# RWKV attention followed by a normalized two-layer MLP on one core: r of the first twelve tiles loaded in long runs and turned by small selection products, rstd on ScalarE, and a new order of the work

## The chip, the cores and the metric

One core of one Trainium2 chip runs the whole program. The metric is device microseconds from start to end of one launch. Five engines work side by side, each with a queue of its own: TensorE (PE, with its weight loads shown apart as PEld), VectorE (DVE), ScalarE (ACT), GpSimd (POOL) and SyncE (SP, which here only issues DMAs). Transfers run on 16 DMA engines.

## The reference

There are 4 batches, 8 heads, 768 steps and a head dimension of 48. Each head carries a 48 x 48 state that decays by w per step; the result, put into rows of 384, goes through a layer normalization with a gain and a two-layer MLP with a residual.

```python
def _attn_ref(r, k, v, w, u):
    for t in range(S):
        cur = np.einsum('bhd,bhe->bhde', u[None] * kt, vt)
        y[:, :, t] = np.einsum('bhd,bhde->bhe', rt, state + cur)
        state = w[None, :, :, None] * state + np.einsum('bhd,bhe->bhde', kt, vt)
...
def _moe_ref(x, g_ln, w_ch1, w_ch2):
    mu = np.mean(x, axis=-1, keepdims=True)
    var = np.mean((x - mu) ** 2, axis=-1, keepdims=True)
    xn = (x - mu) / np.sqrt(var + 1e-06) * g_ln
    ch = np.maximum(xn @ w_ch1, 0.0) @ w_ch2
    return (x + ch).astype(np.float32)
```

w_ch1 is 384 x 1536 and w_ch2 is 1536 x 384. All inputs and the output are float32; the kernel multiplies in bfloat16.

## The kernel before, in words

The sequence is cut into 6 chunks of 128 steps. With 4 batches this makes 24 tiles; tile i is chunk i // 4 of batch i % 4. Tiles 0 to 3 need no state, and tile i reads the state that tile i - 4 left.

**The attention part of a tile.** LR, LK and LV (L328, L325, L331) load r, k and v of the tile with the time step on the partition, all 8 heads side by side: 128 x 8 pieces of 48 float32 numbers, 192 bytes each. SR and SK multiply r by w to the power t (Fr) and k by w to the power -(t+1) (Fk) and write bfloat16, each head padded to 64 (tile sc; L194). TR turns the scaled r and k, four 128 x 128 transposes each, on TensorE (L348), and TC, TCr and TCk copy them from PSUM into trs. From tile 12 on TKR does this turning by a DMA transpose instead (K_BY_DMA, L497). AT multiplies turned k with turned r per head (L371, 48 rows of the array, the two heads of a pair on its two halves), AM masks the result (L381), Q multiplies r by k elementwise, and S forms the u term (L402) and the new state's sum of k times v (L415). CC, ZU and ZD take these out of PSUM, VB multiplies v by the u term per head (L434), Y adds state times r (L444) and A times v (L452), and X adds Vb and gives the sum of each row (L459).

**The MLP part.** SQ gives the squared deviation of a row (L466), XN the centred row in bfloat16, LT or LT2 turns it (TensorE or DMA), UP is the first layer (L527), RL its relu out of PSUM (L543, L545), DN the second layer (L557), OT scales by the row's rstd and adds x (L615), and STO stores. RS makes rstd on GpSimd with a multiply-add (L480) and a power of -0.5 (L483). GROUPS says which tiles go through the first layer together: single tiles for 0 to 5 and 20 to 23, pairs between. The first layer's weights are loaded in thirds (LW1, L301) and scaled by -g to bfloat16 (SW, L308 and L312); the second layer's come into the same three buffers later (LW2, CW).

**The order.** PLAN is a list of steps "name, tile, engine or place". It is issued in this order by hand, so each engine's queue holds its own steps of the list in the order of the list; v, s and g mean VectorE, ScalarE and GpSimd, and h, p, o and a are PSUM pools. SLOTS gives the number of buffers of each ring. All loads and most stores are issued by SyncE, one after the other. DU steps are products of zeros that only keep TensorE busy.

Of the kernel before, what the change touches and what calls it, by code (L numbers as in the profile page):

```python
# [17 lines left out]
PLAN = """
LR,1,- LK,0,- MI,0,g MW,0,v WF,0,s WB,0,- LC,0,s LC,1,s MM,0,g MP,0,v TL,0,s LC,2,s DU,21,h LN,0,s FK,0,s FR,0,s SK,0,v LK,1,- LR,0,- SK,1,v CT,0,o
DU,7,h SR,0,v TR,0,h TCk,0,s SR,1,v TR,1,h TCk,1,v TCr,0,s Q,0,v AT,0,- CP,0,s WL,0,s LR,2,- SR,2,g TCr,1,v LK,2,- SK,2,g TR,2,h AMb,0,v AMa,0,v  # L20
AT,1,- LV,1,- LK,3,- AMb,1,v AMa,1,v UW,0,g TCk,2,s TCr,2,s AT,2,- AMb,2,v UGC,0,s LV,0,- CV,0,s S,0,h CC,0,v VB,0,v ZU,0,v Y,0,h X,0,v XN,0,v LR,3,-
CV,1,s Q,1,g SK,3,g SR,3,g TR,3,- Q,2,g S,1,o CC,1,v VB,1,g ZU,1,v AMa,2,v Y,1,- X,1,v LK,5,- LR,4,- SR,4,g TCr,3,s TCk,3,s AT,3,- Q,3,v AM,3,v LV,2,-
CV,2,s S,2,h CC,2,s ZU,2,v LT,0,o XN,1,s XT,0,s LK,4,- LR,5,- SR,5,v VB,2,v SK,4,g DU,3,p TR,4,- TC,4,v Q,4,v LV,3,- CV,3,s S,3,o CC,3,s SQ,1,s ZU,3,v
LV,4,- SK,5,g TR,5,- TC,5,s VB,3,g Y,2,- X,2,v LT,1,- XT,1,s XN,2,s CV,4,g S,4,h ZU,4,v CC,4,s LV,5,- CV,5,g ATP,4,- AM,4,v LW1,0,- SW,1,s Y,3,h
SQ,0,s X,3,v XN,3,s SQ,2,s LT,2,h XT,2,v Q,5,g S,5,- AM,5,v ZU,5,v Y,4,o SW,2,g SW,0,g UP,16,- RL,16,s LW1,2,- SW,6,s CC,5,s LT,3,- XT,3,s UP,32,-
RL,32,s UP,0,- RL,0,s LW1,1,- SW,5,s VB,4,g X,4,v XN,4,v SW,7,g SW,8,g UP,2,o RL,2,v VB,5,g UP,48,p RL,48,v Y,5,h SW,3,g LK,6,- SK,6,v X,5,v UP,18,-
RL,18,s XN,5,s SW,4,g UP,49,p RL,49,s UP,33,o LR,7,- SR,7,v UP,34,- RL,34,s LK,7,- SK,7,g RS,2,g RL,33,v UP,17,- RL,17,s TR,7,p TC,7,s RS,0,g LT,5,h
XT,5,v LT,4,- UP,1,o LR,6,- Q,7,v LW2,2,- UP,82,- SR,6,g TR,6,- UP,81,- XT,4,s RL,1,v LV,7,- CV,7,v CW,5,v S,7,- CC,7,v ZU,7,v CW,4,g DN,6,- RL,82,v
TC,6,s Q,6,g ATP,6,- AM,7,v AM,6,v LW2,1,- CW,2,s SQ,4,s DN,2,p UP,50,- RL,50,s CW,3,g DN,5,- VB,7,g DN,1,- RL,81,v Y,7,h LW2,0,- CW,1,s CW,0,g DN,4,-
DN,0,- SQ,5,s RS,1,g OT,1,v LV,6,- CV,6,s S,6,h CC,6,s LK,9,- SK,9,g UP,66,o SQ,3,s X,7,v XN,7,g SQ,7,s VB,6,g ZU,6,v RL,66,v UP,64,- RL,64,s Y,6,h  # L30
LR,9,- SR,9,v LR,8,- SR,8,g DN,10,- RS,5,g TR,9,- X,6,v XN,6,s LK,8,- SK,8,v DN,8,- OT,0,v TR,8,- TC,8,v Q,8,v TC,9,s Q,9,v RS,3,g RS,4,g DN,9,-
OT,2,v UP,65,- RL,65,s ATP,8,- UP,80,p AM,9,v LV,9,- CV,9,g LR,10,- SR,10,g DN,18,- S,9,h ZU,9,v DN,17,- CC,9,v LK,10,- SK,10,g LV,8,- CV,8,s S,8,h
LR,11,- SR,11,v CC,8,v RL,80,s ZU,8,v VB,9,g TR,10,- AM,8,v TC,10,v VB,8,g LT2,6,- UP,96,- RL,96,s Q,10,v UP,98,p RL,98,s UP,97,- RL,97,s Y,9,h X,9,v
# [629 lines left out]
```

## Time and profile before

| what | us |
|---|---|
| three runs, median | 148.81 (148.49 to 149.31) |
| profiled execution | 148.24 |
| its span | 146.5 |
| TensorE busy in the span | 135.8 |
| VectorE busy | 110.5 |
| GpSimd busy | 94.0 |
| ScalarE busy | 80.1 |
| DMA queue of SyncE, share of 16 engines | 86.3% |

The span runs from the first to the last instruction of the core. Instructions of DMA issue, branches and semaphores are not counted as busy. In a row of a timeline the first number is the start and the second the duration; xN says how many instructions are merged in it. In a row of the chain of waits the second number is the piece of the chain. In a row of the groups, "busy, mean ns" stands behind the count, then the idle time ahead of the group and what ended it. In a row of a stretch stand the length, then busy time and number of instructions of TensorE, its weight loads, VectorE, ScalarE and GpSimd, then the granted clock of TensorE, the DMA share and GB/s.

### The profile page before, as it was taken

To read this page: it belongs to the slowest core of one execution; us is meant where nothing else is said; L and a number is where in the kernel's file an instruction comes from. 1 tells how busy PE (TensorE), PEld (TensorE's weight loads), DVE (VectorE), ACT (ScalarE), POOL (GpSimd) and SP (SyncE) were. 2 spreads that over 40 slices of the span, in tenths; PEclk is the share of its full clock that TensorE was granted. 3 is DMA by queue.
4 is the path that set the end of the run, shared out by engine and by line. 5 is a ranking of instruction groups with operands and counts; after the bars stand their busy time and mean duration, and the time that the engine had idled before them with its cause. 6 is when DMAs were issued, how large, how long until landed. Compare 5 with 4: busy or idle time off the path is not lost.

```text
span 146.5 us, 4250 instructions
## 1 busy us (share of the span) xinstructions
PE 135.8 (93%) x1693; PEld 108.2 (74%) x1693; DVE 110.5 (75%) x220; ACT 80.1 (55%) x175; POOL 94.0 (64%) x132
## 2 busy tenths in 40 slices
PE   3966699999999999999999999999999999999991
PEld 1455477998687897787688887966877777888871
DVE  4569999767969899985959948897946796875232
ACT  2575577977676467466386560663654752244600
POOL 4089878967888999989957493428553076644030
PEclk9999556999999999999999999999999999999999
DMA  5999899999889999899999999988999997830114
GB/s 97 209 211 221 175 277 401 194 258 380 231 170 188 206 197 232 156 215 242 96 229 206 260 233 186 217 166 185 245 157 199 229 184 156 206 123 0 54 37 182
DMA packets 99267, 28.59 MB, mean 195 GB/s; under 512 B 94508, under 2 KB 97712, under 8 KB 99248
## 3 DMA queue, kind: packets, MB, share of 16 engines
q1 hardware_dynamic: 98352, 27.24, 86.3%
q10 hardware_dynamic: 896, 1.09, 2.0%
q8 instruction: 13, 0.21, 0.6%
q14 instruction: 6, 0.05, 0.1%
HBM read 18.88 MB, written 4.72 MB: 161 GB/s over the span
## 4 chain that ended last, share of the span: by engine, by line
PE 60%; SPq 11%; DMA 11%; DVE 7%; POOL 6%; issue 4%; DVEq 0%; POOLq 0%
PE hp L527 17%; PE o L557 16%; PE s L557 7%; PE s L527 5%; SPq L332 4%; DMA w_f<-in_moe_w_ch_dram 4%; SPq L329 4%; SPq L326 3%; DMA trs<-sc 3%; DMA rf<-in_r_dram 3%; PE o L527 3%; PE at L371 2%; PE hp L452 2%; POOL sc L194 2%; PE at L348 2%
## 5 line engine op out<-in xcount | busy, mean ns | idle before, releaser
L527 PEld LDWEIGHTS <-w_sb 128*128 128x128 bf16 x612 | 47.9, 114 | 2.4 <-POOL w_sb L312 0.4
L527 PE MATMUL hp<-xT,w_sb 128*128 128x128 bf16 (+1 forms) x408 | 39.9, 244 | 0.3 <-POOL w_sb L312 0.3
L557 PEld LDWEIGHTS <-hT 128*128 128x128 bf16 x276 | 25.2, 97 | 13.7 <-issue 0.4
L557 PE MATMUL o<-w_sb,hT 128*128 128x384 bf16 x180 | 34.5, 326 | 0.0
L543 ACT ACTIVATE hT<-hp 128x512 bf16<-128x512 f32 x41 | 24.3, 597 | 18.2 <-PE hp L527 17.7
L381 DVE TENSOR_TENSOR A<-at,mask 128x1024 bf16<-128x1024 f32 (+1 forms) x27 | 28.9, 1096 | 1.2 <-PE at L371 1.2
L194 POOL TENSOR_TENSOR sc<-kf,Fk 128x384 bf16<-128x384 f32 x14 | 14.5, 1044 | 10.5 <-DMA kf<-in_k_dram 10.4
L434 POOL TENSOR_TENSOR Vb<-vf,cc 128x384 f32<-128x384 f32 x17 | 14.7, 868 | 8.7 <-ACT cc L189 3.6
L557 PE MATMUL s<-w_sb,hT 128*128 128x384 bf16 x96 | 18.9, 326 | 0.2 <-DVE x L459 0.2
L194 POOL TENSOR_TENSOR q<-trs 128x512 bf16<-128x512 bf16 x11 | 13.4, 1220 | 5.5 <-PE hp L527 2.6
L194 POOL TENSOR_TENSOR sc<-rf,Fr 128x384 bf16<-128x384 f32 x12 | 13.0, 1082 | 5.3 <-DMA rf<-in_r_dram 5.3
L466 ACT ACTIVATE sqj<-x,sm 128x384 bf16<-128x384 f32 x24 | 14.7, 611 | 1.4 <-DVE x L459 1.3
L615 DVE SCALAR_TENSOR_TENSOR ot<-o,rs,x 128x384 f32<-128x384 f32 x15 | 9.2, 613 | 4.5 <-POOL rs L483 2.8
L459 DVE SCALAR_TENSOR_TENSOR x<-hp,Vb 128x384 f32<-128x384 f32 x19 | 10.5, 554 | 2.3 <-PE hp L452 1.6
L483 POOL TENSOR_TENSOR rs<-rs,expo 128x1 f32<-128x1 f32 (+1 forms) x17 | 10.6, 625 | 1.4
L472 ACT ACTIVATE xn<-x,sm 128x384 bf16<-128x384 f32 x13 | 8.0, 613 | 5.7 <-DVE x L459 5.6
L371 PE MATMUL at<-trs 48*128 48x128 bf16 x192 | 8.6, 229 | 2.4 <-ACT trs L189 1.2
L527 PE MATMUL s<-xT,w_sb 128*128 128x128 bf16 (+1 forms) x120 | 10.8, 235 | 0.0
L194 POOL TENSOR_TENSOR Z<-ZS,WLZ 128x384 bf16<-128x384 f32 x10 | 10.3, 1030 | 0.6 <-DVE ZS L428 0.6
L545 DVE TENSOR_SCALAR hT<-hp 128x512 bf16<-128x512 f32 x9 | 6.2, 689 | 4.6 <-PE hp L527 4.6
L371 PEld LDWEIGHTS <-trs 48*128 48x128 bf16 x192 | 6.0, 99 | 4.9 <-ACT trs L189 2.1
L194 DVE TENSOR_TENSOR sc<-rf,Fr 128x384 bf16<-128x384 f32 x12 | 7.5, 633 | 2.3 <-DMA rf<-in_r_dram 2.2
(116 smaller groups left out, 214.3 us busy)
## 6 DMA issues: line engine op xcount, KB each, us to landing
rf<-in_r_dram SPq DMA_DIRECT2D x24, 192.0 KB, 3.8
kf<-in_k_dram SPq DMA_DIRECT2D x24, 192.0 KB, 3.9
vf<-in_v_dram SPq DMA_DIRECT2D x24, 192.0 KB, 3.9
w_f<-in_moe_w_ch_dram SPq DMA_DIRECT2D x6, 768.0 KB, 7.2
out_dram<-ot SPq DMA_DIRECT2D x18, 192.0 KB, 3.4
out_dram<-ot ACTq DMA_DIRECT2D x5, 192.0 KB, 2.0
trs<-sc SPq DMA_TRANSPOSE x12, 3.9
xT<-xn SPq DMA_TRANSPOSE x9, 2.8
```

The costliest lines, as they stand in the source:

```text
L194: engines[e].tensor_tensor(out=out, in0=in0, in1=in1, op=ALU.mult)
L371: nc.tensor.matmul(out=t[:, par, q, :], lhsT=trs(i)[p0 : p0 + D, 1, q, :], rhs=trs(i)[p0 : p0 + D, 0, q, :], start=True, stop=True,)
L381: nc.vector.tensor_tensor(out=AA(i)[:, a:b].rearrange("p e q t -> p (e q) t"), in0=psum["at", i][:, a:b].rearrange("p e q t -> p (e q) t") ...
L434: engines[e].tensor_tensor(out=Vb(i)[:].rearrange("p (h d) -> p h d", h=H), in0=vf(i)[:], in1=cc(i)[:].unsqueeze(2).to_broadcast([P, H, D] ...
L459: nc.vector.scalar_tensor_tensor(out=xx(i)[:], in0=psum["y", i][:, :C], scalar=1.0, in1=Vb(i)[:], op0=ALU.mult, op1=ALU.add, accum_out=sm[ ...
L466: nc.scalar.activation(out=sqj[:], in_=xx(i)[:], func=ACT.Square, bias=sm[i][:], scale=-float(C), accum_out=sq[g][:, j : j + 1])
L472: nc.scalar.activation(out=xn(i), in_=xx(i)[:], func=ACT.Identity, bias=sm[i][:], scale=-float(C))
L483: nc.gpsimd.tensor_tensor(out=rs[g][:], in0=rs[g][:], in1=expo[:, :n], op=ALU.pow)
L527: nc.tensor.matmul(out=t[:, a * gw : (a + 1) * gw].rearrange("p (j t) -> p j t", j=size), lhsT=w1_sb[n][kc][:, fb::FB], rhs=xT(g)[:, :size ...
L543: nc.scalar.activation(out=o, in_=s, func=ACT.Relu)
L557: nc.tensor.matmul(out=psum["o", i][:, :C], lhsT=hT(g)[:, fk, j * P : (j + 1) * P], rhs=w2_sb[d][:, a, :], start=(seen == 0 and a == 0), s ...
L615: nc.vector.scalar_tensor_tensor(out=ot(i), in0=psum["o", i][:, :C], scalar=rs[g][:, j : j + 1], in1=xx(i)[:], op0=ALU.mult, op1=ALU.add,)
```

## The change

**r of tiles 0 to 11.** LP loads r of two batches of one chunk at once. The partition now holds batch, head and one of 8 blocks of 16 steps, so each of 128 pieces is 16 steps x 48 = 768 numbers, 3072 bytes, contiguous. SP scales it by Fq, w to the power t laid out that way, which WS, LNQ, FA and FQ make at the start (w spread over partitions by a product with a selection matrix, its logarithm, times t, exp). TP turns it: for each of the 16 steps in a block, four products with 64 rows and 64 columns of the array pick the heads of one batch and parity out of the identity (32 moving columns each), 64 products per pair of tiles, into float32 PSUM. TCr copies the result of a tile into trs in the order of time. k of these tiles is turned alone (TK, KC). Heads are paired as h and h + 4 instead of 2q and 2q + 1, which changes the access patterns of SK, SR, CV, CC and Y, not their counts.

**rstd and Vb.** RS becomes two activations on ScalarE, Ln and Exp. VB may run on ScalarE as eight activations, one per head; seven tiles do so.

**The order.** PLAN is written anew; DU is 24 and 8 instead of 21, 7 and 3.

```diff
+PACK = 16
+R_PACKED = 12
-SLOTS = {'kf': 11, 'rf': 11, 'vf': 11, ...}
+SLOTS = {'kf': 10, 'sp': 2, 'rf': 10, 'vf': 10, ...}
-LR,1,- LK,0,- MI,0,g MW,0,v WF,0,s WB,0,- LC,0,s LC,1,s ...
+MI,0,g LP,0,- LP,1,- LK,2,- MW,0,v MM,0,g MS,0,v MR,0,g LK,4,- WF,0,s WB,0,h LC,0,s ...
...
+    def WS(i, e):
+        t = psum["wq"] = bank(e, "p", [P, 512], FP32)
+        for a in range(2):
+            nc.tensor.matmul(
+                out=t[:, :D], lhsT=sel[:, a].rearrange("k b h p -> k (b h p)"),
+                rhs=rows[:HP, a * DP : a * DP + D], start=(a == 0), stop=(a == 1),
+            )
+    def LNQ(i, e):
+        nc.scalar.activation(out=lnq[:], in_=psum["wq"][:, :D], func=ACT.Ln)
+    def FA(i, e):
+        times(
+            e, Fq[:], lnq[:].unsqueeze(1).to_broadcast([P, PACK, D]),
+            pow_r[:].unsqueeze(2).to_broadcast([P, PACK, D]),
+        )
+    def FQ(i, e):
+        nc.scalar.activation(out=Fq[:], in_=Fq[:], func=ACT.Exp)
...
+    def LP2(i, e):
+        c, b = divmod(2 * i, B)
+        issuer(e).dma_start(
+            out=rp(i).rearrange("p j d -> p (j d)"),
+            in_=r[b : b + 2, :, c * L : (c + 1) * L, :].rearrange("b h (p j) d -> (b h) p (j d)", j=PACK),
+        )
+    def SP2(i, e):
+        times(e, sp(i)[:, :, :D], rp(i), Fq[:])
...
     def SK(i, e):
-        times(e, sck(i)[:, :, :D], kf(i)[:], Fk[:])
+        times(e, paired(sck(i))[:, :, :, :D], plain(kf(i)[:]), plain(Fk[:]))
...
+    def TP2(i, e):
+        t = psum["tp", i] = ps_a.tile([P, 2, 512], FP32, name="at")
+        n = HP * LP
+        for j in range(PACK):
+            for par in range(2):
+                for b in range(2):
+                    h0 = b * DP
+                    a = (b + par) % 2
+                    nc.tensor.matmul(
+                        out=t[a * DP : (a + 1) * DP, b, j * n : (j + 1) * n],
+                        lhsT=sp(i)[h0 : h0 + DP, j, :], rhs=ident[h0 : h0 + DP, h0 + a * n : h0 + (a + 1) * n],
+                        start=True, stop=True,
+                    )
+    def TK(i, e):
+        t = psum["tk", i] = bank(e, "a", [P, 2 * HP, P], BF16)
+        flat = sck(i).rearrange("p (q e) d -> p q (e d)", e=2)
+        for q in range(HP):
+            nc.tensor.transpose(out=t[:, q, :], in_=flat[:, q, :], identity=ident[:])
+    def KC(i, e):
+        copy(e, trs(i)[:, 1], psum["tk", i][:, :HP])
     def TCr(i, e):
-        copy(e, trs(i)[:, 0], psum["tr", i][:, :HP])
+        if i < R_PACKED:
+            copy(
+                e, trs(i)[:, 0].rearrange("p q (t j) -> p q t j", j=PACK),
+                psum["tp", i // 2][:, i % 2].rearrange("p (j q t) -> p q t j", j=PACK, q=HP),
+            )
+        else:
+            copy(e, trs(i)[:, 0], psum["tr", i][:, :HP])
...
     def VB(i, e):
...
+        if e == "s":
+            for h in range(H):
+                nc.scalar.activation(out=o[:, h], in_=vf(i)[:, h], func=ACT.Copy, scale=cc(i)[:, h : h + 1])
...
     def RS(g, e):
-        n = GROUPS[g]
-        nc.gpsimd.tensor_scalar(
-            out=rs[g][:], in0=sq[g][:], scalar1=1.0 / C, scalar2=1e-6 * C * C, op0=ALU.mult, op1=ALU.add
-        )
-        nc.gpsimd.tensor_tensor(out=rs[g][:], in0=rs[g][:], in1=expo[:, :n], op=ALU.pow)
+        nc.scalar.activation(out=rs[g][:], in_=sq[g][:], func=ACT.Ln, bias=eps[:], scale=1.0 / C)
+        nc.scalar.activation(out=rs[g][:], in_=rs[g][:], func=ACT.Exp, scale=-0.5)
```

How the instructions move is shown at three places. The first is SyncE's queue at the start of the program; rf, kf and vf with a number are r, k and v of a tile (rf0 in the change: of tiles 0 and 1), w1_f a third of the first layer's weights. Before, the last of 18 tile loads and the weights:

```order
L329 DMA rf4_84<-in_r_dram 128x8x48
L332 DMA vf2_93<-in_v_dram 128x8x48
L326 DMA kf4_73<-in_k_dram 128x8x48
L329 DMA rf5_85<-in_r_dram 128x8x48
L332 DMA vf3_94<-in_v_dram 128x8x48
L332 DMA vf4_95<-in_v_dram 128x8x48
L332 DMA vf5_96<-in_v_dram 128x8x48
L301 DMA w1_f0_243<-in_moe_w_ch1_dram 128x3x512
```

The change, from the queue's first load:

```order
L388 DMA rf0_79<-in_r_dram 128x1x768
L388 DMA rf1_80<-in_r_dram 128x1x768
L381 DMA kf2_71<-in_k_dram 128x8x48
L381 DMA kf4_73<-in_k_dram 128x8x48
L381 DMA kf0_69<-in_k_dram 128x8x48
L397 DMA vf1_87<-in_v_dram 128x8x48
L381 DMA kf3_72<-in_k_dram 128x8x48
L381 DMA kf1_70<-in_k_dram 128x8x48
L397 DMA vf2_88<-in_v_dram 128x8x48
L397 DMA vf0_86<-in_v_dram 128x8x48
L388 DMA rf2_81<-in_r_dram 128x1x768
L356 DMA w1_f2_242<-in_moe_w_ch1_dram 128x3x512
```

The first weights stand behind 18 tile loads before, and behind 8 tile loads and three loads of packed r after; r of six tiles, k of five and v of three are then on their way, instead of all three of six tiles.

The second place is VectorE's queue from its first scaling on; sc holds scaled r and k, sp scaled packed r, A a masked tile. Before:

```order
L194 TENSOR_TENSOR sc0_102<-kf0_69,Fk_232 128x8x48
L194 TENSOR_TENSOR sc1_103<-kf1_70,Fk_232 128x8x48
L194 TENSOR_TENSOR sc0_102<-rf0_80,Fr_231 128x8x48
L194 TENSOR_TENSOR sc1_103<-rf1_81,Fr_231 128x8x48
L191 COPY trs1_113<-hp_325 128x512
L194 TENSOR_TENSOR q0_117<-trs0_112 128x512
```

The change:

```order
L211 TENSOR_TENSOR sc2_98<-kf2_71,Fk_230 128x2x4x48
L211 TENSOR_TENSOR Fq_227<-lnq_228,pow_r_225 128x768
L211 TENSOR_TENSOR sc4_100<-kf4_73,Fk_230 128x2x4x48
L211 TENSOR_TENSOR sc0_96<-kf0_69,Fk_230 128x2x4x48
L211 TENSOR_TENSOR sp0_84<-rf0_79,Fq_227 128x16x48
L211 TENSOR_TENSOR sp1_85<-rf1_80,Fq_227 128x16x48
L211 TENSOR_TENSOR sc3_99<-kf3_72,Fk_230 128x2x4x48
L208 CAST trs0_106<-at_343 128x512
```

Six scalings and the making of Fq stand ahead of the queue's first copy out of PSUM, where four scalings stood.

The third place is rstd of the first groups; sq is the squared deviation, rs the result. Before, on GpSimd:

```order
L434 TENSOR_TENSOR Vb2_138<-vf6_97,cc1_124 128x384
L194 TENSOR_TENSOR sc3_105<-rf8_88,Fr_231 128x8x48
L480 TENSOR_SCALAR rs5_214<-sq5_196 128x1
L483 TENSOR_TENSOR rs5_214<-rs5_214,expo_229 128x1
L194 TENSOR_TENSOR sc0_102<-rf10_90,Fr_231 128x8x48
```

The change, on ScalarE:

```order
L572 ACTIVATE sqj_201,sq0_184<-x0_134,sm0_160 128x384
L585 ACTIVATE rs0_202<-sq0_184,eps_222 128x1
L586 ACTIVATE rs0_202<-rs0_202 128x1
L206 CAST w2_sb0_252<-w1_f0_240 128x768
L206 CAST trs4_110<-at_1136 128x512
```

Two instructions of GpSimd between scalings become two of ScalarE behind the squares that they need.

More of the change, by code (lines that the diff above doesn't have):

```diff
@@ L20 @@
[L20 to L27, printed above, removed]
@@ L93 @@
     FB = FW // P
+    LP = L // PACK
+    assert 2 * H * LP == P and B % 2 == 0
     assert D <= DP and H % 2 == 0 and S % L == 0 and C % P == 0 and F % (P * NW) == 0
@@ L118 @@
     kf = ring("kf", [P, H, D], FP32)
-    rf = ring("rf", [P, H, D], FP32)
+    rf2 = [const.tile([P, 2, H, D], FP32, name=f"rf{a}") for a in range(SLOTS["rf"] // 2)]
+    sp = ring("sp", [P, PACK, DP], BF16)
     vf = ring("vf", [P, H, D], FP32)
```

148 lines of the change are left out of this document (94 added, 54 removed).

## The prediction

> **What bounds the kernel now.** I read the page first (engine shares, slices), then the chain of work that ended last, then busy times by stretch.
>
> ```profile
> span 146.5 us, 4250 instructions
> PE 135.8 (93%) x1693; PEld 108.2 (74%) x1693; DVE 110.5 (75%) x220; ACT 80.1 (55%) x175; POOL 94.0 (64%) x132
> PEclk9999556999999999999999999999999999999999
> DMA  5999899999889999899999999988999997830114
> ```
>
> TensorE is busy 93% of the span; the clock row shows the one stage in which it was held back, slices 4 to 6 (about 14 to 25 us). The DMA engines are near full until 130 us. The chain says which of the two counts where:
>
> ```profile
> 16.70 0.98 SPq L332
> 17.72 5.84 DMA w_f<-in_moe_w_ch_dram
> 23.67 1.38 POOL w_sb L312 x2
> 25.10 0.86 PE hp L527 x12
> ...
> 71.88 4.84 DMA trs<-sc
> ...
> 90.52 4.70 DMA rf<-in_r_dram
> ...
> 142.48 1.00 PE o L574 x12
> ```
>
> To 25.10 us the chain is SyncE's queue issuing 18 loads of r, k and v, then the first third of w1 landing 5.84 us after its issue at 17.72, then its scaling; from 25.10 on it is mostly TensorE, to 143.48. So there are two stages. The start does not wait for DMA alone, though:
>
> ```profile
> 6.00:12.00 6.00, 4.33 (x63) 3.31 (x62) 4.72 (x10) 3.91 (x11) 4.29 (x6) 1.00 1.07 212
> 12.00:18.00 6.00, 4.12 (x62) 3.13 (x60) 5.93 (x15) 2.89 (x7) 5.47 (x6) 0.67 0.96 192
> 18.00:24.00 6.00, 5.55 (x72) 4.51 (x73) 5.88 (x12) 3.79 (x9) 4.58 (x7) 0.50 1.00 315
> ```
>
> The third busy column is VectorE: 5.93 and 5.88 of 6 us. An earlier w1 helps only as far as VectorE gets a first tile ready earlier.
>
> How full is the second stage? A busy matmul is not a matmul at its peak, so I count products at the pace that the chain shows where they follow without a gap:
>
> ```profile
> 28.81 0.17 PE hp L444 x4
> 28.98 0.20 PE hp L452 x8
> ...
> 32.54 0.45 PE s L348 x8
> ...
> 36.00 0.08 PE s L402 x4
> ...
> 36.26 0.17 PE s L415 x4
> 36.43 0.65 PE o L557 x4
> 37.08 0.55 PE at L371 x16
> ...
> 38.39 0.67 PE hp L527 x12
> ...
> 51.47 0.66 PE hp L527 x6
> ```
>
> That is 42 ns (96 columns), 25 (48 columns), 56 (a turning of 128 columns), 20 (2 columns), 42 (96), 162 (384), 34 (L371, 48 rows by 128 columns), 56 (128) and 110 (256). The counts follow from the code. First layer: 360 x 56 + 252 x 110 = 47.9 us. Second: 24 x 12 x 162 = 46.7. L371: 192 x 34 = 6.5. Turnings: (96 + 24) x 56 = 6.7. S: 96 x 20 + 80 x 42 + 4 x 162 = 5.9. Y: 80 x 42 + 192 x 25 = 8.2. Together 121.9 us. Before 25.10 TensorE had done, of useful work, 57 turnings (3.2), A of tiles 0 to 5 (1.6), S of 0 to 5 (1.8) and Y of 0 to 4 (1.2): 7.8 us. So 114.1 us were left for the 118.4 us from 25.10 to 143.48; only 4.3 us were empty there. The kernel is a start of 25 us and then a TensorE stream 96% full. Every microsecond of products added to that stream is a microsecond of time.
>
> **The change part by part.** *The start.* Rates first (the last two columns are DMA share and GB/s):
>
> ```profile
> 1.00:2.00 1.00, 0.00 (x0) 0.00 (x0) 0.97 (x8) 0.00 (x0) 0.89 (x7) 1.00 0.07 13
> 2.00:3.00 1.00, 0.70 (x1) 0.49 (x2) 0.31 (x3) 0.22 (x1) 0.21 (x1) 1.00 0.99 194
> 23.00:24.00 1.00, 1.00 (x18) 0.84 (x17) 1.00 (x2) 0.35 (x1) 0.34 (x2) 0.50 1.06 412
> ```
>
> The same stage in the timeline of VectorE and GpSimd:
>
> ```profile
> 5.31 1.03 DVE L194 TENSOR_TENSOR sc<-kf,Fk 128x384 bf16<-128x384 f32 x2 [3.00 <-ACT Fk L277]
> 7.49 1.00 POOL L194 TENSOR_TENSOR sc<-rf,Fr 128x384 bf16<-128x384 f32 x1 [5.28 <-DMA rf<-in_r_dram]
> ```
>
> Data flow from 2.0 us. A tile in 192-byte runs (196.6 KB) takes 0.93 us at 212 GB/s; w1, in 2048-byte runs, moves at 412. The fifth load landed at 7.5 us, 0.9 after 2.0 + 5 x 0.93. The trace has no 3072-byte load: between 212 GB/s (1.86 us for two tiles of r) and w1's 412 (0.96); I take 0.96, the nearer run length. k of tile 2, third in the new queue, then lands at 2.0 + 2 x 0.96 + 0.93 + 0.9 = 5.8 us (the first k scaling began at 5.31 before), and the first third of w1 at 2.0 + 3 x 0.96 + 8 x 0.93 + 1.9 + 0.9 = 15.1, against 23.6 now. So w1 stops being what comes last; VectorE's row of work is next:
>
> ```profile
> 9.98 3.07 DVE L381 TENSOR_TENSOR A<-at,mask 128x512 bf16<-128x512 f32 x5
> 13.63 0.55 DVE L194 TENSOR_TENSOR Z<-hp,WLZ 128x384 bf16<-128x384 f32 x1
> 14.10 0.55 DVE L459 SCALAR_TENSOR_TENSOR x<-hp,Vb 128x384 f32<-128x384 f32 x1
> 14.69 0.42 DVE L474 TENSOR_SCALAR xn<-x,sm 128x384 bf16<-128x384 f32 x1
> ```
>
> and, from the groups by form,
>
> ```profile
> L545 DVE TENSOR_SCALAR hT<-hp 128x512 bf16<-128x512 f32 x9 | 6.2, 689 | 4.6 <-PE hp L527 4.6
> L191 DVE COPY trs<-hp 128x512 bf16<-128x512 bf16 x2 | 0.8, 418 | 1.0 <-PE hp L348 1.0
> L194 DVE TENSOR_TENSOR q<-trs 128x512 bf16<-128x512 bf16 x13 | 6.9, 541 | 1.7 <-DMA trs<-sc 0.9 <-ACT trs L189 0.7
> ```
>
> From the scaling of k of tile 2 to the copy of tile 2's turned xn, VectorE has 28 instructions: eight of 384 elements at 0.47 us (the start-to-start step 13.63 to 14.10), 3.8; three X at 0.58, 1.7; Fq and two scalings of packed r, 768 elements, at twice 0.47, 2.8; six half masks at 0.61, 3.7; three copies of turned k at 0.42, 1.3; one copy of turned r from float32 at 0.69, 0.7; one q 0.5; two small copies and xT 0.6. Sum 15.1, so 20.9 us from 5.8. Exp of Fq on ScalarE is mostly covered by two k scalings (0.2 us shows). I add 0.8 for waits, about what VectorE waited there before (1.0 for turnings, in the row of L191), and place the first w1 product at 21.7. The rest hides, just: after the second q GpSimd has r of tiles 4 and 5 (2 x 1.00), two w1 scalings (1.38), xn, q and v of tile 3 (about 2.5), and ends near 20.5; late by a microsecond it would cost that microsecond. Gain: 25.1 - 21.7 = **-3.4 us**; bounds -4.2 (no waits) and -1.5.
>
> *The stream.* Removed: 48 turnings of r, 2.7 us. Added: six turnings of packed r, 64 products each, of unknown price p. Before the first w1 product the new order has done less: 20 turnings of k, six of xn, A and S of four tiles, Y of three: 4.2 us beside three packed turnings. Left over: 121.9 - 2.7 - 4.2 + 3p = 115.0 + 3p, against 114.1: **+0.9 us + 3p**.
>
> The price p: no product of 64 rows, 64 columns and 32 moving columns is in the trace. If each takes its turn, like L452's 48 columns, 64 x 25 ns = 1.6 us; at 34 ns it would be 2.2. L371's 34 ns, against 56 for a whole-array product of as many columns, show two products on different halves of the rows running side by side; alternating halves, as the new loop does, 64 products make 32 pairs of 25 ns, 0.8 us. Four side by side would give 0.4. I take 0.8, since L371 is the nearest case, and keep 0.4 and 2.2. So **+2.4 us**.
>
> The Trainium skill, "TensorE: Matmul & The Clock Gate", "What overlaps and what doesn't", says that weight loads overlap running products only where the row group differs. L371's pace agrees. Its page "TensorEngine Tiling (Array Packing)", "Restrictions", says that column tiling disables the fast weight load, which speaks against this change; no run here shows that yet. With the first page's 64 / 1.2 = 53 ns a load and 32 loads for each half of the rows, p would be 1.7 us, an estimate, and the sum +2.7 us higher.
>
> *The empty 4.3 us.* rstd leaves GpSimd:
>
> ```profile
> L483 POOL TENSOR_TENSOR rs<-rs,expo 128x1 f32<-128x1 f32 (+1 forms) x17 | 10.6, 625 | 1.4
> L194 POOL TENSOR_TENSOR q<-trs 128x512 bf16<-128x512 bf16 x11 | 13.4, 1220 | 5.5 <-PE hp L527 2.6
> ```
>
> The waits, and a small activation in ScalarE's timeline:
>
> ```profile
> DVE ot L615 <- POOL rs L483: 2.8, 4, 1.0
> ```
>
> ```profile
> 9.14 0.20 ACT L291 ACTIVATE ln_p<-cols 128x4 f32<-128x4 f32 x1
> ```
>
> Off GpSimd go 10.6 us and four waits of VectorE, 2.8 us; ScalarE gets 34 activations at 0.20, 6.8 us, and with Vb by eight activations on seven tiles 56 x 0.20 = 11.2 more, on an engine that is 55% busy. DMA saves 12 x 0.93 - 6 x 0.96 = 5.4 us, and two transfers of nearly 5 us are on the chain (71.88 and 90.52). Against that, q moves to GpSimd for three tiles (1.22 instead of 0.54) and copies of turned r and k come in two pieces. Behind a longer ScalarE queue stand the relu evictions that free PSUM for the first layer. I give **-1.3 us**, bounds -3.5 and +1.0. The heads' new pairing only strides reads by 48-element runs: nothing, up to 0.05 us an instruction, hidden outside the start.
>
> Sum: -3.4 + 0.9 + 2.4 - 1.3 = **-1.4 us**. The profiled execution took 148.24 us (span 146.5, 1.74 outside it), 0.57 below the median of the three runs, 148.81; the sum is made on its span, the difference carried to the median: **147.4 us**.
>
> **The rivals.** R1, the turnings serialize. The 64 products take 25 to 34 ns each; p is 1.6 to 2.2, the sum +1.0 to +2.8 us, 149.8 to 151.6, say **150.7**, slower. It decides from p = 1.27 us (20 ns a product), where the sum is zero. For it: nothing in the trace uses half the columns. Against: L371's pairs. The Trainium skill's rule on column tiling, above, would have this mechanism and, by its estimate of 1.7 us, 150.1. R2, the stream closes up: start at 21.0 and only 1.5 us empty, -4.1 + 0.9 + 2.4 - 2.8 = -3.6, **145.2**. For it: the two DMA waits and rstd on the chain. R3, the start is not earlier than 23.6: GpSimd's 2 us for r of tiles 4 and 5 stand ahead of w1's scaling, and TensorE may still be at the 0.50 clock; then -1.5 + 0.9 + 2.4 - 1.0 = +0.8, **149.6**. R4, the change does not do what it says: packed r moves at 212 GB/s, k of tile 2 lands 1.8 us later, VectorE starts so much later, and DMA saves nothing: -1.6 + 0.9 + 2.4 - 0.2 = +1.5, **150.3**.
>
> **How the numbers follow.** Forecast 0.42, R1 0.22, R2 0.18, R3 0.13, R4 0.05. About 0.5%, 0.75 us, is what a measurement of this kernel can tell from no change. The forecast's own spread, 146.5 to 148.6, lies four fifths on the faster side and R2 all: 0.34 + 0.18, less a little of R2's doubt, 0.48. Same: 0.08 of the forecast and half of R3 with what was taken off: 0.18. Slower: 0.34. The range, 145.0 to 151.0, holds R2's middle, R1's lower half and R3.
>
> **What would show it.** Right: first w1 product near 21.7 us; w1 landed by 16; packed turnings of about 0.8 us; no GpSimd rstd in front of the outputs; under 3.5 us empty in the stream. Wrong: turnings above 1.3 us, packed r landing as late as two tiles, VectorE waiting in the start, or evictions waiting behind Vb on ScalarE.

## The result, and the profile after

The changed kernel takes **154.62 us** (median of 4 runs, 152.92 to 155.02) against 148.97 (148.49 to 149.31) for the kernel before on the same chip: ratio 1.036, 95% interval 1.0276 to 1.0444. It is slower by 5.65 us; the forecast was 147.4 us, in a range of 145.0 to 151.0. The profiled execution took 155.02 us. Ratios, here and below, stand against the kernel before on the same chip and leave out executions more than 1.5% above a kernel's fastest, which leaves e4 none.

The page of the changed kernel, against 146.5 us, 135.8 us of PE and half clock in slices 4 to 6 before:

```profile
span 153.2 us, 4976 instructions
PE 138.4 (90%) x2028; PEld 110.5 (72%) x2028; DVE 117.4 (77%) x241; ACT 94.8 (62%) x256; POOL 78.0 (51%) x94
PEclk9999955999999999999999999999999999999999
```

TensorE is busy only 2.6 us longer, the span is 6.7 us longer: most of the loss is time in which TensorE does nothing.

**The start.** k of tiles 2 and 4 (the issue and its time to landing), then VectorE's timeline, then TensorE's:

```profile
L381 SPq DMA_DIRECT2D kf<-in_k_dram x2: 573/584/595, 2.1 to 2.7; - x2
DMA to landing us min/median/max: 5.5/5.6/5.7
```

```profile
7.68 0.56 DVE L211 TENSOR_TENSOR sc<-kf,Fk 128x384 bf16<-128x384 f32 x1 [3.52 <-ACT cols L206]
...
13.88 0.69 DVE L208 CAST trs<-at 128x512 bf16<-128x512 f32 x1 [1.57 <-ACT trs L206]
```

```profile
8.69 2.77 PE L296 MATMUL at<-warm 128*128 128x512 bf16 x6
...
12.24 1.50 PE L429 MATMUL at<-ident,sp 64*64 64x32 bf16 x128
13.68 0.40 PE L439 MATMUL hp<-ident,sc 128*128 128x128 bf16 x4
...
24.17 1.48 PE L630 MATMUL hp<-xT,w_sb 128*128 128x128 bf16 x12
```

k, issued at 2.1 us behind 786 KB of packed r, landed 5.6 us later, at 7.7, not at 5.8. VectorE starts at 7.68 (its row names ScalarE's copy of cols, which ended just then, at 7.66; in e4, below, the same row stands at 7.72 and names the load of k). It later waits 1.57 us for a turned copy. The first w1 product comes at 24.17 us (25.10 before, 21.7 forecast). The two packed turnings, 128 products, take 12.24 to 13.68 us. And the first w1 products still run at half clock; two stretches with the granted clock behind the five busy columns:

```profile
20.00:25.00 5.00, 4.50 (x108) 3.73 (x109) 4.90 (x13) 3.81 (x11) 5.00 (x7) 0.50 1.12 292
25.00:30.00 5.00, 4.50 (x74) 4.20 (x72) 3.94 (x7) 3.23 (x6) 4.44 (x5) 0.84 0.87 164
```

Before, the clock was back at 24.2 us (0.77 over 24.0 to 24.5), ahead of the stream; here at 26.6, 2.4 us into it.

**The stream.** TensorE's timeline from 30 us on, and the first product of two tiles at once (256 columns):

```profile
30.33 1.50 PE L630 MATMUL hp<-xT,w_sb 128*128 128x128 bf16 x24 [0.63 <-DVE x L565]
...
33.13 0.69 PE L429 MATMUL at<-ident,sp 64*64 64x32 bf16 x64 [0.19 <-DVE A L481]
33.75 0.34 PE L615 MATMUL hp<-ident,xn 128*128 128x128 bf16 x3
...
39.27 0.34 PE L549 MATMUL o<-Z,trs 128*128 128x96 bf16 x4 [0.36 <-issue]
...
44.65 1.47 PE L660 MATMUL o<-w_sb,hT 128*128 128x384 bf16 x8 [0.98 <-DVE Z L211]
```

```profile
61.04 1.47 PE L630 MATMUL hp<-xT,w_sb 128*128 128x256 bf16 x12
```

64 products of a packed turning take 33.13 to 33.75, 0.62 us. The brackets are empty time. To have all of it, I took the start of each product to the start of the next, less the price of the product at the forecast's paces (9.7 ns for a packed one). In the kernel before, the stream from 25.1 to 143.3 us holds 114.1 us of products and 4.1 us empty, near the forecast's 4.3; 0.7 of it lies before 50 us. In the change, from 24.2 to 150.0 us, it holds 116.9 us of products and 8.9 empty, 5.2 of it before 50 us, and about 1.2 of that is the half clock. (Products of 2 columns start 25 to 28 ns apart, not the 20 that the forecast read; with that, both counts of empty time fall by 0.4 us.) The second layer's first product stands at 44.65 us; before, it was at 36.3. So the end of the stream moved by 6.6 us: start -0.9, products +2.8, empty time +4.7.

What TensorE waits for before 45 us is not one engine. Two pieces of the chain, VectorE and then ScalarE:

```profile
30.28 0.47 DVE q L211
30.75 1.20 DVE hT L648 x2
31.95 1.13 DVE A L481
33.08 0.33 DVE q L211
33.41 0.48 DVE Z L211
...
40.53 0.60 ACT hT L646
41.13 0.72 ACT w_sb L206
41.86 0.50 ACT hT L646
42.35 0.70 ACT w_sb L206
```

In the second, relu (hT) and the copies of the second layer's weights (w_sb) take turns. From 44.65 to 62 us the chain is TensorE's again but for 1.9 us of VectorE around 55.

### The profile page after: what moved, and what is told of

It reads as the page before. It is cut to its first block, busy times and chain, and to the rows that moved or that the text cites. A ratio compares the mean times of both kernels' runs of the same rounds, so it can differ in the third digit from the quotient of the medians.

```text
span 153.2 us, 4976 instructions
## 1 busy us (share of the span) xinstructions
PE 138.4 (90%) x2028; PEld 110.5 (72%) x2028; DVE 117.4 (77%) x241; ACT 94.8 (62%) x256; POOL 78.0 (51%) x94
## 3 DMA queue, kind: packets, MB, share of 16 engines
q1 hardware_dynamic: 86736, 27.24, 86.5%
## 4 chain that ended last, share of the span: by engine, by line
PE 65%; DVE 13%; DMA 12%; issue 3%; ACT 3%; POOL 1%; SPq 1%; ACTq 0%; DVEq 0%; POOLq 0%
PE hp L630 16%; PE o L660 11%; PE s L660 11%; PE o L630 5%; DVE A L481 4%; PE s L630 4%; PE at L471 4%; DMA rf<-in_r_dram 3%; DMA trs<-sc 3%; DMA rows<-in_moe_g_ln_dram 3%; DMA out_dram<-ot 3%; PE hp L558 2%; PE at L296 2%; DVE Z L211 1%; DVE q L211 1%
## 5 line engine op out<-in xcount | busy, mean ns | idle before, releaser
L646 ACT ACTIVATE hT<-hp 128x512 bf16<-128x512 f32 x35 | 20.8, 595 | 13.6 <-PE hp L630 13.1
L660 PE MATMUL s<-w_sb,hT 128*128 128x384 bf16 x144 | 27.5, 326 | 0.0
L660 PE MATMUL o<-w_sb,hT 128*128 128x384 bf16 x132 | 25.2, 326 | 1.0 <-DVE Z L211 1.0
L211 POOL TENSOR_TENSOR Vb<-vf,cc 128x384 f32<-128x384 f32 x10 | 8.6, 860 | 26.2 <-ACT cc L206 9.1
L718 DVE SCALAR_TENSOR_TENSOR ot<-s,rs,x 128x384 f32<-128x384 f32 x12 | 7.4, 615 | 8.0 <-PE s L660 5.7
L540 ACT ACTIVATE Vb<-vf,cc 128x48 f32<-128x48 f32 x56 | 13.3, 322 | 0.4 <-DVE cc L208 0.3
L630 PE MATMUL o<-xT,w_sb 128*128 128x128 bf16 (+1 forms) x132 | 12.9, 244 | 0.4 <-DMA xT<-xn 0.4
L211 POOL TENSOR_TENSOR sc<-rf,Fr 128x384 bf16<-128x384 f32 x9 | 9.8, 1099 | 2.7 <-DMA rf<-in_r_dram 2.7
L646 ACT ACTIVATE hT<-o 128x512 bf16<-128x512 f32 x10 | 5.9, 594 | 7.4 <-PE o L630 7.3
L211 DVE TENSOR_TENSOR sc<-kf,Fk 128x384 bf16<-128x384 f32 x10 | 6.2, 627 | 3.8 <-ACT cols L206 3.5
```

The costliest lines, as they stand in the source:

```text
L211: engines[e].tensor_tensor(out=out, in0=in0, in1=in1, op=ALU.mult)
L540: nc.scalar.activation(out=o[:, h], in_=vf(i)[:, h], func=ACT.Copy, scale=cc(i)[:, h : h + 1])
L630: nc.tensor.matmul(out=t[:, a * gw : (a + 1) * gw].rearrange("p (j t) -> p j t", j=size), lhsT=w1_sb[n][kc][:, fb::FB], rhs=xT(g)[:, :size ...
L646: nc.scalar.activation(out=o, in_=s, func=ACT.Relu)
L660: nc.tensor.matmul(out=psum["o", i][:, :C], lhsT=hT(g)[:, fk, j * P : (j + 1) * P], rhs=w2_sb[d][:, a, :], start=(seen == 0 and a == 0), s ...
L718: nc.vector.scalar_tensor_tensor(out=ot(i), in0=psum["o", i][:, :C], scalar=rs[g][:, j : j + 1], in1=xx(i)[:], op0=ALU.mult, op1=ALU.add,)
```

## The experiments

Executions of one kernel spread by up to 5.8 us here (the kernel before beside e7: 146.74 to 152.53), so medians are compared beside the ratios, and each trace is one execution. At first there were three theories. **S**: the loss is made in the first 45 us of the new order. **P**: packing r costs it, by its turnings and what waits for them. **A**: rstd and Vb hold up ScalarE's queue.

**e1, the new order with plain r.**

```diff
-LP,0,- LP,1,- LK,2,- ... SP,0,v TP,0,- ... FA,0,v FQ,0,s
+LR,0,- LR,1,- LR,2,- LR,3,- LK,2,- ... SR,0,v SR,1,v TP,0,- ...
```

TP is then eight 128 x 128 transposes of the two tiles in place of the 64 products.

> The new order with nothing packed: each packed load, scaling and turning is replaced at its place by those of its two tiles in 192-byte runs (scaling by Fr, eight 128x128 turnings), and the making of Fq is gone. Kernel before about 149.0 us, the change about 154.5. Theory S (the loss is the new order's first 45 us: k late, zeros ahead of the first turnings, VectorE and ScalarE behind): it stays, 152.5 to 156. Theory P (packing costs: its products, its two-piece copies, its longer scalings): 150.5 or less. Theory A (rstd and Vb on ScalarE hold up its queue): 152.5 or more, since both stay.

151.75 us (151.28 to 153.05), ratio 1.0258 [1.0173, 1.0343]: between S and P. The larger part of the loss stays without packing; packing takes about 1.5 us by the ratios, 2.9 by the medians. By the same count, e1's stream has 116.4 us of products, nearly the change's, and 6.3 us empty, against 8.9: by these two traces, what packing costs is waits, not products. VectorE's first scaling here:

```profile
7.81 1.15 DVE L200 TENSOR_TENSOR sc<-kf,Fk 128x384 bf16<-128x384 f32 x2 [5.20 <-DMA kf<-in_k_dram]
```

k of tile 2 stands behind the same 786 KB, as four plain loads instead of two packed ones, and arrives at the same time (7.68 in the change). So packed r moves no faster: the change's transfers reached 341 GB/s from 3 to 4 us, e1's 221, but it began with 114 against 196 from 2 to 3 us and fell to 240 and 202 in the next two. The queue line of both pages (packets, MB, time of the packets as a share of the span), the change first:

```profile
q1 hardware_dynamic: 86736, 27.24, 86.5%
```

```profile
q1 hardware_dynamic: 98352, 27.24, 83.8%
```

With 12% fewer packets the change's transfers took 86.5% of 153.2 = 132.5 us, e1's 83.8% of 149.5 = 125.3. Packing saved no transfer time over the whole run either.

**e2, the old order with packed r,** rstd on GpSimd.

```diff
-LR,1,- LK,0,- ... SR,0,v TR,0,h ... TC,4,v
+LP,0,- LK,0,- ... SP,0,v TP,0,- TK,0,h ... TCr,4,v TCr,5,v KC,4,v
```

> The old order with r of tiles 0 to 11 packed: a pair's load, scaling and turning stand where the first of its two tiles had them; rstd stays on GpSimd and Vb where it was. Theory S: 149 to 151, since the stream gets six turnings of 0.65 us for 2.7 us of old turnings, and the start some waits for Fq. Theory P: 153 or more. Theory A: 149 to 150.5, since nothing moves to ScalarE.

161.28 us (160.32 to 161.87), ratio 1.0881 [1.0797, 1.0965]. Its first w1 product, and around 55 us VectorE and GpSimd:

```profile
31.45 1.15 PE L628 MATMUL hp<-xT,w_sb 128*128 128x128 bf16 x12
```

```profile
54.72 3.16 DVE L201 TENSOR_TENSOR q<-trs 128x512 bf16<-128x512 bf16 x2
```

```profile
54.63 1.84 POOL L201 TENSOR_TENSOR sp<-rf,Fq 128x768 bf16<-128x768 f32 x1
```

The start is 6.3 us later (a tile's turning now waits for its partner's load and scaling too), and about 6 us are lost from 56 to 66 us: 2.9 in two waits for VectorE, most of the rest because the granted clock was 0.50 from 59.4 to 66.3 us. P's figure is met, but by waiting, not by the turnings; in this order packing does not fit.

**e3 and e8, the change with rstd (and Vb) back on GpSimd.**

```diff
-RS,0,s ... VB,2,s VB,1,s
+RS,0,g ... VB,2,g VB,1,g      (e8: RS alone)
```

> The change with rstd back on GpSimd (multiply-add and power) and Vb of the seven tiles on GpSimd in place of ScalarE, at the same places of the list. Theory A: 151 or less. Theories S and P: 153 to 156; GpSimd gets back what it had, and the first 45 us hardly change but for two Vb of 1.9 us.

> The change with rstd alone back on GpSimd; Vb of seven tiles stays on ScalarE. With both back the time was 166.9 us. If the power on GpSimd (0.62 us each, 17 of them) is what that order can't hold, 160 to 167 us; if Vb is, 153 to 156 us; if rstd on ScalarE holds up relu evictions, as theory A had it, 150 to 153.

e3: 166.94 us (165.95 to 169.19), 1.1247 [1.1152, 1.1343]. e8: 162.66 us (161.6 to 165.34), 1.0963 [1.0893, 1.1033]. e3 is far above every theory's range. Theory A falls for the new order: ScalarE is where it needs rstd. GpSimd's group in e8:

```profile
L578 POOL TENSOR_SCALAR rs<-sq 128x1 f32<-128x1 f32 (+1 forms) x17 | 3.4, 202 | 18.4 <-ACT sqj L563 17.4
```

The time is where the expectation put the power's price, but the power takes what it took before (0.62 us each). What is new is its place: the new list has RS mostly right behind the square, so GpSimd's queue stands 17.4 us waiting for squares (6.6 in the same group before), scalings behind it.

**e5, the kernel before with rstd on ScalarE,** at the same places of the list.

```diff
-        nc.gpsimd.tensor_scalar(... op0=ALU.mult, op1=ALU.add)
-        nc.gpsimd.tensor_tensor(... op=ALU.pow)
+        nc.scalar.activation(... func=ACT.Ln, bias=eps[:], scale=1.0 / C)
+        nc.scalar.activation(... func=ACT.Exp, scale=-0.5)
```

> The kernel before with nothing changed but rstd: Ln and Exp on ScalarE at the places where GpSimd had it. Theory A: 151 or more. Theories S and P: 148 to 149.5; at most a small gain from the four waits of VectorE for GpSimd's rstd, 2.8 us in all.

150.96 us (150.24 to 151.74), 1.0208 [1.0122, 1.0295]. VectorE's waits for rstd, 2.8 us in four waits before, are now:

```profile
DVE ot L612 <- ACT rs L480: 5.5, 6, 1.5
```

In the old order the move costs about 2.5 us, near theory A's figure, where I had counted it as a gain. Part of it may be the half clock, which in this profile lasts to 27.6 us, 2.1 us into the stream.

**e4, e6, e10: the start, made earlier.** e4 leaves out the zero products, e6 loads k of tiles 2 and 4 first, e10 does both.

```diff
-LP,0,- LP,1,- LK,2,- ... LK,4,- ... DU,24,a ... DU,8,a
+LK,2,- LK,4,- LP,0,- LP,1,- ...
```

> The change without its two steps of zero products (24 and 8). In the trace of the change the 24 zeros hold TensorE from 8.69 to 11.25 us, while scaled k of tile 4 was ready at about 9.6, so three turnings and the first two packed turnings stand behind them. Theory S (the loss is in the new order's first 45 us): the turnings move up by 1.0 to 1.6 us, the first w1 product from 24.2 to 23.0 to 23.6, and the time falls to 153.2 to 154.2 us, unless the clock of TensorE falls earlier and stays low in the stream. Rival P (the packing itself costs it): no change, 154.3 to 155.0. A third way: without the zeros the half clock covers more of the stream, and the time rises by 0.5 to 1.5 us.

> The change with k of tiles 2 and 4 loaded ahead of packed r of tiles 0 to 3, nothing else moved. The first scaling of VectorE came at 7.68 us in the change, because k of tile 2 stands behind 768 KB of packed r; here k should land at about 5.0 and the first scaling start at 5.3 to 5.8. Theory S: VectorE's row of work bounds the start, so the first w1 product comes 1 to 2 us earlier (22.2 to 23.2) and the time falls to 152.8 to 153.7 us. If the zeros behind the first turning, or packed r that now lands later, take the place of k, the first w1 product stays at 24.2 and the time at 154.6. Rival P: no change.

> The change with k of tiles 2 and 4 loaded first and without the zero products. Theory S: both obstacles gone, the first w1 product at 21.7 to 22.7 us, as the prediction had it, and the time 152.0 to 153.2 us. If the earlier start is lost again to the half clock and to waits between 24 and 50 us, the first w1 product is as early, and the time stays above 153.8. Rival P: 154 to 155.

e4 154.56 us (151.07 to 155.71); e6 154.35 (153.3 to 157.42), 1.0418 [1.0331, 1.0506]; e10 154.05 (152.77 to 155.24), 1.0393 [1.0292, 1.0495]. First w1 product and first paired product, e4 and then e10:

```profile
23.39 1.48 PE L619 MATMUL hp<-xT,w_sb 128*128 128x128 bf16 x12
...
61.47 1.47 PE L619 MATMUL hp<-xT,w_sb 128*128 128x256 bf16 x12
```

```profile
22.84 1.48 PE L619 MATMUL hp<-xT,w_sb 128*128 128x128 bf16 x12
...
61.05 1.47 PE L619 MATMUL hp<-xT,w_sb 128*128 128x256 bf16 x12
```

The start moved, by 0.8 us in e4 as S said and by 1.3 in e10, a little less than S said: VectorE's first scaling came at 5.22 us there, but it then waited 1.94 us for k of tile 0. By 61 us nothing of the gain is left; e10's median is 0.6 us below the change's. The traces hold the same products in the same order and can be compared one by one: e10 is 1.2 us ahead of the change at 36 us, 0.9 at 51 and level from 57 on. What it runs into there is VectorE; the chain of e10:

```profile
47.62 1.29 DVE q L200
...
49.65 1.06 DVE ot L707 x2
50.71 1.64 DVE vv L197
52.35 1.13 DVE A L470
```

e6's profiled execution was its longest, 157.42 us. Its first w1 product came at 23.42 us (22.2 to 23.2 expected), but the granted clock fell to 0.50 a second time, from 44.4 to 47.8 us, and the first paired product came at 63.86.

**e23, the start made later.**

```diff
-SW,2,s UP,34,-
+SW,2,s DU,16,o UP,34,-
```

> The change with four more zero products of 512 columns just ahead of the first w1 product, which hold TensorE for 0.9 to 1.7 us there. Theory W (TensorE has too little prepared work until about 60 us, the other engines set the pace, and the moment at which the stream starts is worth nothing): the time stays at 154 to 155 us and the first paired product at 61 us. Rival F (the stream is full, as the prediction had it): both come 0.9 to 1.7 us later, 155.5 to 156.3 us.

154.38 us (153.71 to 154.88), 1.037 [1.0297, 1.0443]:

```profile
25.79 1.07 PE L619 MATMUL hp<-xT,w_sb 128*128 128x128 bf16 x12
...
61.36 1.47 PE L619 MATMUL hp<-xT,w_sb 128*128 128x256 bf16 x12
```

1.6 us later at the start, 0.3 at 61 us, nothing at the end: not F's 155.5 to 156.3. But the clock gave back about 0.9 of the 1.6 us: it returned at 26.3 us, much as in the change (26.6), so that only 0.5 us of this stream ran at 0.50 instead of 2.4. The rest went in waits between 27 and 45 us. Against the spread of the executions, 0.7 us alone would hardly show, so e23 supports theory W and does not prove it; e4 and e10, whose gains can be followed until they are gone, carry it.

**e7, the kernel before with w1 three loads earlier.**

```diff
-LV,3,- ... LV,4,- ... LV,5,- ... LW1,0,-
+LW1,0,- LV,3,- ... LV,4,- ... LV,5,-
```

> The kernel before with one step moved: the first third of w1 is loaded ahead of v of tiles 3, 4 and 5 instead of behind them. If the landing of w1 alone bounds the start, as the chain of the kernel before has it, the first w1 product moves from 25.1 to 22.3 to 23.0 us and the time falls by 1.5 to 2.5 us, to 146 to 147. If VectorE's row bounds it as well, the first product moves by under 1 us and the time by under 0.7. If v of tiles 3 to 5, now later, delays their states, the time rises by up to 1 us.

149.19 us (148.15 to 151.94, 10 runs), 1.0055 [1.0004, 1.0105]:

```profile
26.49 0.86 PE L516 MATMUL hp<-xT,w_sb 128*128 128x128 bf16 x12
```

With v of three tiles later, the first w1 product came 1.4 us *later* than before (25.10), and yet the last group of the stream starts at 142.2 us, against 142.3 before; the time rose by half a per cent, hardly clear of the noise. Product by product, the delay is still 1.1 us at 60 us, 0.5 at 80 and gone at 120; the empty time fell from 4.1 us to 2.7. So a microsecond at the start was not a microsecond of time in the old order either.

**e15 and e18, the two orders joined** near 50 us: e15 the old order and then the new (plain r, rstd and Vb on ScalarE from the join), e18 the new one (packed) and then the old.

```diff
 PLAN = before's steps up to UP,96, then the change's remaining ones      (e15)
 PLAN = the change's steps up to DN,10, then before's remaining ones      (e18)
```

> The kernel before with its own order for the first 311 steps (about the first 51 us) and, from there, the remaining steps in the order of the change, with rstd and the Vb steps of that part on ScalarE as the change has them; r is never packed. Theory S (the loss is made in the first 50 us of the new order): as fast as before, 148 to 149.7 us. Rival L (the later part costs as well, by rstd and Vb on ScalarE or by its order): 150.5 us or more; rstd on ScalarE alone, in the old order, cost 2.5 us.

> The change with its own order and packed r for the first 292 steps (about the first 50 us), and from there the remaining steps in the order of the kernel before, with rstd and Vb of that part on GpSimd; the last pair of tiles is still packed. Theory S: as slow as the change, 153 to 155.5 us. Rival L: a good part of the loss goes, 148.5 to 151.5 us.

e15: 153.68 us (153.0 to 154.24), 1.0379 [1.0321, 1.0436]. e18: 159.11 (157.4 to 160.27), 1.0675 [1.0583, 1.0767]. By its time e15 speaks for L, but its chain at the join does not:

```profile
52.94 0.39 DVE trs L182
53.33 3.37 DMA out_dram<-ot
56.72 0.63 DVE ot L616
```

VectorE waits there 1.1 us for a store to free a buffer of output rows, which neither order does at this place. By my count e15 has 0.4 us empty up to 51 us, 6.3 from 51 to 64, and 1.9 in the rest, with rstd and Vb of that part on ScalarE: the later part of the new order runs as full as the old one's (3.2 us from 64 us on). Of the 6.3 us, 3.0 are waits of TensorE; most of the rest is the clock, granted at 0.50 from 56.1 to 63.0 us. Behind such a stall the other engines can get ahead, so this is support, not proof. e18 has 8.1 us empty up to 61 us (the change 5.9), and 5.4 behind (the change 3.0), where TensorE waits for a copy of v, a turned tile and an output. Joining lists costs more than the question was worth.

**e11, e20, e21, e22: less work for GpSimd and ScalarE.** e11 is e10 with the scalings of packed r of tiles 4 to 11 on VectorE; e20 leaves these four scalings out, e21 makes Vb on ScalarE in one activation, e22 does both. What e20 to e22 leave out is not computed.

```diff
-SP,2,g ... SP,3,g ... SP,4,g ... SP,5,g
+SP,2,v ... SP,3,v ... SP,4,v ... SP,5,v      (e11; none of them in e20, e22)
-            for h in range(H): nc.scalar.activation(out=o[:, h], ... scale=cc(i)[:, h : h + 1])
+            nc.scalar.activation(out=o, ... scale=cc(i)[:, 0:1])      (e21, e22)
```

> The change with k of tiles 2 and 4 loaded first, without the zero products, and with the scalings of packed r of tiles 4 to 11 on VectorE instead of GpSimd (four instructions). With k first and no zeros alone the time was 154.05 us, and single instructions of VectorE that read and write only SBUF took up to 1.4 us longer while GpSimd scaled packed r for 1.83 us. Theory H (these held-up instructions make the waits of TensorE between 24 and 60 us): they go, VectorE gets 4 x 0.95 us more, of which most was lost before, and the time falls to 151.5 to 153.2 us. Rival V (VectorE is simply full there): the 3.8 us come on top and the time rises to 155 to 158 us.

> The change without the four scalings of packed r on GpSimd (tiles 4 to 11 turn the scaled r of tiles 0 to 3 again, so r of those tiles is not what is computed). This takes 4 x 1.83 us from GpSimd, and the hold-ups of VectorE beside it. Theory H (packing's cost beyond its turnings is this scaling): the time falls by 1.5 to 3 us, to 151.5 to 153. If the waits lie elsewhere: 154 to 155.

> The change with one activation instead of eight for each Vb on ScalarE (all heads scaled by the factor of head 0, so Vb of seven tiles is not what is computed). This takes 7 x about 1.4 us from ScalarE. Theory A2 (ScalarE's eight small activations hold up the start and the copies behind them): 152 to 153.5 us. If they hide: 154 to 155.

> Both of the two: no later scaling of packed r and one activation for each Vb on ScalarE (the same parts are not computed). If the losses add up, 150 to 152 us; if another engine takes over at once, no better than the better of the two.

The idea came from the change's timelines, VectorE and then GpSimd:

```profile
27.42 2.19 DVE L211 TENSOR_TENSOR Vb<-vf,cc 128x384 f32<-128x384 f32 x1
```

```profile
27.36 1.83 POOL L211 TENSOR_TENSOR sp<-rf,Fq 128x768 bf16<-128x768 f32 x1
```

An instruction of 0.55 us takes 2.19 while GpSimd scales packed r, and the 0.63 us wait at 30.33 follows from it. e11: 158.46 us (157.92 to 160.03), 1.0721 [1.0643, 1.0798]; TensorE now waits for VectorE's scalings:

```profile
PE at L418 <- DVE sp L200: 6.3, 5, 2.5
```

e20: 154.01 us (151.88 to 155.01), 1.0259 [1.014, 1.0379]. e21: 154.76 (154.05 to 157.48), 1.0383 [1.0298, 1.0467]. e22: 154.27 (153.39 to 154.91), 1.0354 [1.0262, 1.0445]. For e11 theory V is right in kind (158.46 stands just above its 155 to 158), and H fails; by e20's median it fails there too. Taking 7 us of work from GpSimd and 9 from ScalarE at the same time (e22) gains nothing measurable; e20's ratio is lower, but e22's, which contains it, is not.

**e24 and e25, the second layer's weights earlier,** with three copies on GpSimd; e25 with e10's start.

```diff
-LV,7,- ... LV,4,- ... LW2,1,- CW,2,s ... CW,3,s ... LW2,2,- CW,5,s
+LW2,1,- LW2,2,- LV,7,- ... LV,4,- ... CW,2,g ... CW,3,g ... CW,5,g
```

> The change with the loads of two thirds of the second layer's weights four loads earlier in SyncE's queue (about 4 us), and three of their copies to bfloat16 on GpSimd, which was idle from 40.0 to 43.7 us, instead of ScalarE. Theory D (TensorE lacks ready products between 38 and 45 us because the second layer starts at 44.7 us): its first product comes 1 to 3 us earlier, the 1.1 us of empty time ahead of it goes, and the time falls by 1 to 2 us, to 152.6 to 153.6. Rival: k and r of later tiles, now behind these loads, take it back, 154 to 155.5 us.

> The same, with k of tiles 2 and 4 loaded first and no zero products (together 154.05 us without the earlier weights). If the second layer's late start was what made the earlier start worthless, the gains now add up: 151 to 152.5 us. If another wait before 60 us takes its place, 153.5 to 155.

e24: 158.25 us (157.67 to 158.47), 1.0646 [1.059, 1.0701]. e25: 157.12 (155.22 to 158.46), 1.0533 [1.0444, 1.0622]. GpSimd in e24:

```profile
37.27 1.03 POOL L197 CAST vv<-vf 128x384 bf16<-128x384 f32 x2 [1.91 <-DMA vf<-in_v_dram]
...
40.76 1.81 POOL L200 TENSOR_TENSOR sp<-rf,Fq 128x768 bf16<-128x768 f32 x1 [2.46 <-DMA rf<-in_r_dram]
```

v and packed r, now behind 1.6 MB of weights, come too late; the turning behind that scaling waits 1.4 us, and the granted clock falls to 0.50 from 44.5 to 47.9 us. The second layer's first product, which was to come 1 to 3 us earlier, comes at 46.7 us instead of 44.65. Theory D fails, and the loss is more than the rival's 154 to 155.5: where one load moves up, others move back.

## Why the prediction was wrong

The sum was -3.4 (start) + 3.3 (products) - 1.3 (empty time) = -1.4 us. Measured on the stream: -0.9, +2.8, +4.7.

**The failing step** is the empty time, with the model behind it: "a start of 25 us and then a TensorE stream 96% full", carried over to a new order, where the empty 4.3 us were expected to shrink by 1.3. The count was right for the kernel before (4.1 us). The rule drawn from it, that a microsecond at the start or of products is a microsecond of time, was not: in its trace e7 lost 1.4 us at the start of the old order and nothing at the end. In the new order 8.9 us are empty. There the first w1 product at 22.84, 23.39, 24.17 or 25.79 us gave the first paired product at 61.05, 61.47, 61.04 or 61.36, and 154.05 to 154.62 us (e10, e4, the change, e23). The prediction's own working held the warning: it counted that the new order "has done less" before the first w1 product (A and S of four tiles, not six) and charged only the products. What it missed is that these were a reserve: finished work that TensorE can turn to while VectorE, ScalarE or a load is late. The change begins its stream with a smaller one, and its second layer, the other work to turn to, starts at 44.65 us instead of 36.3.

**The empty time**, -1.3 forecast, is +4.7: the largest miss, and 4.5 of it lies before 50 us. I read it as what rstd's removal and shorter transfers would free. rstd: the waits for it do go from GpSimd, but ScalarE's queue is no shorter (e5: +2.5 us in the old order). Its activations and those of Vb, 0.20 us each by the forecast, took

```profile
L540 ACT ACTIVATE Vb<-vf,cc 128x48 f32<-128x48 f32 x56 | 13.3, 322 | 0.4 <-DVE cc L208 0.3
...
L585 ACT ACTIVATE rs<-sq,eps 128x1 f32<-128x1 f32 (+1 forms) x17 | 4.9, 290 | 1.6 <-DVE ot L718 1.4
L586 ACT ACTIVATE rs<-rs 128x1 f32<-128x1 f32 (+1 forms) x17 | 3.5, 203 | 0.5
```

21.7 us in all instead of 18.0: Vb's last 0.32 us each and overlap, 0.24 from one to the next. Leaving out seven eighths of Vb's gained nothing measurable (e21). In the new order the move is needed (e8). Transfers: the 5.4 us of DMA that packed r was to save did not appear (e1).

**The start**, -3.4 forecast, is -0.9. k of tile 2 came at 7.7 us instead of 5.8, as rival R4 had it. From there VectorE's row to the copy of tile 2's turned xn took 15.8 us with its waits, to 23.5, and the forecast had 15.9: the sum is right, though the 1.57 us wait is twice the 0.8 allowed and the work was shorter. From that copy to the first w1 product TensorE ran A and S of tile 3 at half clock, 0.7 us that the sum does not have. 1.9 and 0.7 us are the 2.5 that are missing. The first third of w1, issued at 11.7 us, took at least 6.2 us to land, so it came near 18 us or later, not at 15.1; GpSimd scaled packed r until 19.9 and had not to wait for it. R3's condition, not earlier than 23.6, was met; its half clock too, 2.4 us of the stream. But R3's 149.6 and R4's 150.3 charged these to a full stream and stayed 4 to 5 us short.

**The products** were right in size. p is 0.62 us, near the 0.8 taken from L371's pairs; with it the term is 0.9 + 3 x 0.62 = +2.8, as counted. The mechanism was not quite the pairs: the records start four products 3 to 4 ns apart, one on each quarter of the array, and the next four 22 ns later. R1 (1.6 to 2.2 us) is refuted. So is the estimate from the Trainium skill, 1.7 us by "TensorE: Matmul & The Clock Gate", "LDWEIGHTS (loading the stationary operand)", and "TensorEngine Tiling (Array Packing)", "Restrictions": where the trace and the pages differ, 9.7 ns a product decides. R2, the stream closing up to 1.5 us, went the other way: 8.9 us are empty.

**What stays open.** Whether the small reserve is the reason. The chain shows VectorE and ScalarE in turn ahead of TensorE before 45 us, and VectorE again where TensorE comes earlier (e10). Leaving out packing took off 1.5 to 2.9 us (e1). No other single suspect carried the loss: each removal (zeros, late k, GpSimd's scaling, Vb in eight steps) left 154 us, and two repairs (scaling on VectorE, weights earlier) made it 157 to 158. That the small reserve is the reason agrees with all of these and with e15; no run restores the reserve within the new order, so it is argued, not shown. Nothing tried beats the kernel before.

## What to carry to other kernels

Before a gain at the start of a pipeline is booked, ask how much finished work the busiest engine will have in reserve when it begins, and move that engine's start by itself, later as well as earlier: if a microsecond of delay is free, as in e7, so may be a microsecond of gain. Follow the shift product by product, and look at the clock, which gave back 0.9 of e23's 1.6 us. A count of "96% full" belongs to one order of the work, and even there it does not say that the start sets the end. And an engine's small steps are priced with what stands in the queue behind them: the same rstd cost 2.5 us on ScalarE in one list and 8 us on GpSimd in the other.
